# Spreading the pooling logits' maximum over all partitions by a store to DRAM and a load, in place of a diagonal, two products with ones and a copy

## The chip, the cores and the metric

The kernel runs on one core of one Trainium2 chip. What counts is the device time of one execution in microseconds (us). The kernel before was timed in three runs; one further execution was recorded by the hardware profiler, and every trace row below comes from that execution. Engine names are those of the profile: PE is TensorE (PEld its weight loads), DVE is VectorE, ACT is ScalarE, POOL is GpSimd, and SP is SyncE, which here only issues DMAs.

## The reference, cut to what matters

```
batch, n_heads, seq, head_dim = 8, 8, 576, 64;  n_mem = 32
a   = phi - max(phi, axis=2)                 # per (batch, head, memory slot), over the sequence
a   = exp(a);  a = a / (sum(a, axis=2) + 1e-9)
k_m = einsum('bhsm,bhsd->bhmd', a, k)        # pooling: 576 keys become 32
v_m = einsum('bhsm,bhsd->bhmd', a, v)
scores = q @ k_m^T / sqrt(64);  attn = softmax(scores)
x   = (attn @ v_m), heads side by side       # 4608 x 512
h   = x @ w_in                               # 512 -> 2048
out = (h - tanh(h)) @ w_out                  # 2048 -> 512
```

The change concerns the first line of the pooling softmax alone: the maximum of `phi` over the 576 positions, for each of the 256 pairs of head and memory slot of one batch, and how that maximum reaches the place where it is subtracted.

## The kernel before, in words

The 4608 tokens are cut into 18 units of 256. For each unit `u` and each quarter `fb` of the 2048 hidden features there is one slot: `mm1` (L572, into the PSUM tile `hs`), a polynomial for h - tanh(h) that goes ACT, DVE, ACT, DVE, ACT, POOL (L579, L587, L592, L597, L603, L608), three sums for a fast product on DVE (`f`, L621), and the second product (`mm2_blocks`, L708 and L715), which works on the slot two back. Values are split in a high and a low half of 16 bits, so there are several products for each. The first part of the kernel (up to about 225 us) is written out word by word in `START`. From then on a loop runs over slots 18 to 71, and `tasks` says which attention steps of a batch go into which slot.

A slot has three places for such steps: `do(0)` after `mm1`, `do(1)` after `mm2_blocks`, `do(2)` at the end of the slot. `PLAN` gives the steps of batches 4 to 7 by slot, counted from the slot of the batch's first token (36, 44, 52 and 60): in a string, words ahead of `;` go to the first place, words behind `;` to the second, words behind `|` to the third. `in_order` ties every engine to the order in which the program issues its instructions, so an engine, the DMA issue on SP included, never passes a waiting instruction.

The steps of one batch that matter here:

- `FQ`, `FA` (-11): the logits are loaded twice, as `pt` (partition = pair, 576 positions along the row, L102, into a buffer of the ring `q`, which has two) and as `e` (partition = position, 256 pairs along the row, L106).
- `X` (-10, second place): DVE takes the maximum of each row of `pt` (`mx`, 128 partitions by 2, L146) and multiplies the identity by it (`dg`, a diagonal for each of the two halves, L148).
- `KR..0` (same place, behind `X`): SP issues the first two key/value loads (L126, ring `q`) and the tail `kt` (L119).
- `XP` (-9, third place): one matrix product of a matrix of ones with `dg` (L157) puts the 256 maxima on every partition of the PSUM tile `pmx`. In the trace it is two pairs of weight load and product, since the operands are 32 bits.
- `YM` (same place): ACT copies `pmx` to the SBUF tile `ms` (L178), and POOL subtracts it from `e` in three instructions (L162 and twice L168).
- `YE` (-8, second place): ACT takes the exponential of `e` (L182).
- `V..0`, `KR..1`, `V..1` (-7): PE pools keys and values (`pkv`, L220 and L228). The second two key/value loads reuse the buffers of the first two, so SP issues them once `V..0` has read those.

Batches 0 and 1 subtract the maximum in another layout, and batches 2 and 3 are issued by `START` and `PLAN3`; none of these four is touched. The PSUM tile `pmx` comes from the pool `ps_a`, which has one buffer, shared with `pkv`, `pp` (L524) and others. The tiles `dg`, `ms` and the second half of a batch's queries share the one SBUF buffer of tag `qt`.

Of the kernel before, what the change touches and what calls it, by code (L numbers as in the profile page):

```python
# [8 lines left out]
F32 = mybir.dt.float32  # L9
# [4 lines left out]
AF = mybir.ActivationFunctionType  # L14
# [4 lines left out]
P = 128  # L19
# [66 lines left out]

class Attention:


    def __init__(self, tc, c, big, ps_a, ins):  # L90
        self.tc, self.c, self.big, self.ps_a, self.ins = tc, c, big, ps_a, ins
# [51 lines left out]
    def top(self, b, d):  # L143
        nc, big = self.tc.nc, self.big
        mx = big.tile([P, 2], F32, tag="mx", name=f"mx{b}")
        nc.vector.tensor_reduce(mx, d["pt"], axis=AX.X, op=ALU.max)  # L146
        dg = big.tile([P, 2, P], F32, tag="qt", name=f"dg{b}", bufs=1)
        nc.vector.tensor_tensor(  # L148
            dg, self.c["ident"].unsqueeze(1).to_broadcast((P, 2, P)),
            mx.unsqueeze(2).to_broadcast((P, 2, P)), op=ALU.mult,  # L150
        )
        d["dg"] = dg

    def top_all(self, b, d, ps=None):
        nc, dg = self.tc.nc, d["dg"]
        pa = self.psum(f"pmx{b}", ps)
        nc.tensor.matmul(pa[:, 0, 0:256], self.c["ones"], dg.rearrange("p a b -> p (a b)"), start=True, stop=True)  # L157
        d["px"] = pa
# [15 lines left out]

    def expo_pool(self, b, d):

        m = self.big.tile([P, 256], F32, tag="qt", name=f"ms{b}", bufs=1)
        self.tc.nc.scalar.activation(m, d["px"][:, 0, 0:256], AF.Copy)  # L178
        self.less_top(self.tc.nc.gpsimd, d["e"], m)

    def expo_exp(self, b, d):
        self.tc.nc.scalar.activation(d["e"], d["e"], AF.Exp)  # L182
# [155 lines left out]
def split_path(ctx, tc, c, ins, out):  # L338
    nc = tc.nc
# [5 lines left out]
    ps_o = ctx.enter_context(tc.tile_pool(name="ps_o", bufs=1, space=PSUM))  # L345
    ps_a = ctx.enter_context(tc.tile_pool(name="ps_a", bufs=1, space=PSUM))
    dram = ctx.enter_context(tc.tile_pool(name="part", bufs=1, space=bass.MemoryType.DRAM))
# [3 lines left out]
    wout_hi = const.tile([P, 16, DM], F16, name="wout_hi")  # L351
    wout_lo = const.tile([P, 16, DM], F16, name="wout_lo")
    att = Attention(tc, c, big, ps_a, ins)

    RING = {"gg": 3, "h3": 2, "uu": 2, "q": 2, "sc": 2}
    raws = {}
# [131 lines left out]
    st = [dict() for _ in range(B)]  # L488
# [306 lines left out]
    def early(b):  # L795
        return ps_early if b == 0 else None

    def cubic(u, fb, stay):
# [11 lines left out]
        "KA": lambda b: att.load_kv(b, st[b], (0,)), "KB": lambda b: att.load_kv(b, st[b], (1,)), "Q": lambda b, t: att.load_q(b, st[b], t, "q"), "QT": lambda b, t: att.load_q(b, st[b], t, "qt"),  # L810
        "KR": lambda b, r: att.load_kv_half(b, st[b], r),
        "X": lambda b: att.top_bias(b, st[b]) if b < N_ROWS else att.top(b, st[b]), "YX": lambda b: att.expo_rows(b, st[b]),
        "XT": lambda b: att.expo_turn(b, st[b], early(b), ps_o), "XP": lambda b: att.top_all(b, st[b], early(b)),
        "Y": lambda b: att.expo(b, st[b]), "YM": lambda b: att.expo_pool(b, st[b]), "YE": lambda b: att.expo_exp(b, st[b]),
        "V": lambda b, r: att.pool_half(b, st[b], r, st[b]["pk"] if r else None), "N": lambda b, r=None: att.norm(b, st[b]) if r is None else att.norm_half(b, st[b], r),
        "U": lambda b: att.turn(b, st[b], early(b)), "UV": att_turn_v, "W": att_window,
# [24 lines left out]
    for word in START.split():  # L841
        if ":" in word:
            k, tag = word.split(":")
# [3 lines left out]


    PLAN = (
# [241 lines left out]
@with_exitstack  # L1091
def tile_kernel(ctx: ExitStack, tc: tile.TileContext, qt, kva, kvt, pha, phx, w_in, w_out, out):
    nc = tc.nc
    ins = dict(qt=qt, kva=kva, kvt=kvt, pha=pha, phx=phx, w_in=w_in, w_out=w_out)
    const = ctx.enter_context(tc.tile_pool(name="const", bufs=1))
    c = {"first": len(nc.cur_bb.bb.instructions)}
    for name, shape, dt in (
        ("ident", [P, P], F32), ("ones", [P, P], F32), ("ones16", [P, 1], F16), ("one", [P, 1], F32),
        ("beta", [P, 1], F32), ("idw", [P, P], F32), ("nidp", [P, P], F16), ("idw", [P, P], F32), ("nid16", [P, P], F16), ("stat", [P, N_CHECK], F32), ("bad", [P, 1], I32),
    ):  # L1100
        c[name] = const.tile(shape, dt, name=name)
    make_identity(nc, c["ident"])
    nc.vector.tensor_scalar(c["nid16"], c["ident"], -1.0, None, op0=ALU.mult)
    nc.vector.tensor_scalar(c["nidp"], c["ident"], -S_V * S_W / S_P, None, op0=ALU.mult)
    nc.vector.tensor_scalar(c["idw"], c["ident"], S_W, None, op0=ALU.mult)
    nc.gpsimd.memset(c["ones"], 1.0)
    nc.gpsimd.memset(c["ones16"], 1.0)
    nc.gpsimd.memset(c["one"], 1.0)
    nc.gpsimd.memset(c["beta"], BETA)
    with ExitStack() as inner:  # L1110
        split_path(inner, tc, c, ins, out)
    with tc.If(c["wide"] > 0):
        with ExitStack() as inner:
            wide_path(inner, tc, c, ins, out)
# [39 lines left out]
```

## Time and profile before

| | |
|---|---|
| median of 3 runs | 659.96 us (659.03 to 661.41) |
| profiled execution: own time | 659.43 us |
| profiled execution: span of the trace | 657.6 us |
| granted PE clock, mean | 0.995 |
| busy DVE, ACT, POOL over the span | 523.6, 375.8, 251.0 us |
| bytes moved by DMA | 84.98 MB |

The span reaches from the first to the last recorded instruction; the execution's own time is 1.83 us longer. A timeline row gives the start in us, how long the row's instructions took together (first start to last end), engine, line, operation, the tile written and the tiles read, and how many instructions the row holds; in brackets stands how long the engine was idle just before, and what ended that. Matmuls overlap, so a row of one product lasts longer than the step to the next product's start.

### The profile page before, as it was taken

To read this page: it belongs to the slowest core of one execution; us is meant where nothing else is said; L and a number is where in the kernel's file an instruction comes from. 1 tells how busy PE (TensorE), PEld (TensorE's weight loads), DVE (VectorE), ACT (ScalarE), POOL (GpSimd) and SP (SyncE) were. 2 spreads that over 40 slices of the span, in tenths; PEclk is the share of its full clock that TensorE was granted. 3 is DMA by queue.
4 is the path that set the end of the run, shared out by engine and by line. 5 is a ranking of instruction groups with operands and counts; after the bars stand their busy time and mean duration, and the time that the engine had idled before them with its cause. 6 is when DMAs were issued, how large, how long until landed. Compare 5 with 4: busy or idle time off the path is not lost.

```text
span 657.6 us, 15599 instructions
## 1 busy us (share of the span) xinstructions
PE 642.2 (98%) x6690; PEld 456.3 (69%) x6690; DVE 523.6 (80%) x790; ACT 375.8 (57%) x509; POOL 251.0 (38%) x173
## 2 busy tenths in 40 slices
PE   8889999999999999999999999999999999999996
PEld 4355656566557777777776677877687777887885
DVE  6899999999855787875898679777978686867773
ACT  4577686666424456545655466545654677666541
POOL 0225141222222245451535353624452555455531
PEclk9899999999999999999999999999999999999999
DMA  9999345301423301324331515142415333234201
GB/s 343 377 365 393 109 170 180 117 3 65 146 97 102 138 28 74 113 91 145 105 113 66 168 51 168 37 162 70 146 41 197 98 101 117 63 117 136 86 33 37
DMA packets 25996, 84.98 MB, mean 129 GB/s; under 512 B 2880, under 2 KB 2880, under 8 KB 25152
## 3 DMA queue, kind: packets, MB, share of 16 engines
q1 hardware_dynamic: 24624, 81.55, 35.9%
q10 hardware_dynamic: 1296, 2.36, 0.9%
q8 instruction: 54, 0.88, 0.6%
q14 instruction: 22, 0.18, 0.1%
HBM read 72.37 MB, written 11.53 MB: 128 GB/s over the span
## 4 chain that ended last, share of the span: by engine, by line
PE 79%; DVE 11%; DMA 4%; ACT 2%; issue 2%; POOL 1%; SPq 0%; DVEq 0%; ACTq 0%; POOLq 0%
PE hs L572 20%; PE x L715 13%; PE o L708 13%; PE o L715 10%; PE o L651 6%; PE h L572 4%; PE o1h L651 3%; PE pp L524 3%; DMA raw<-in_w_out_dram 2%; PE pkv L220 2%; DMA kv<-in_kva_dram 2%; PE warm L789 1%; DVE wt L384 1%; DVE h L597 1%; DVE h L587 1%
## 5 line engine op out<-in xcount | busy, mean ns | idle before, releaser
L608 POOL TENSOR_TENSOR g<-h,g 128x1024 f16<-128x1024 f32 x64 | 138.5, 2165 | 327.3 <-ACT g L603 233.3
L572 PEld LDWEIGHTS <-ph 128*128 128x128 f16 x2304 | 176.9, 98 | 20.5 <-issue 6.0
L572 PE MATMUL hs<-ah,ph 128*128 128x256 f16 (+3 forms) x1152 | 151.5, 246 | 0.0
L587 DVE SCALAR_TENSOR_TENSOR h<-hs,u 128x1024 f32<-128x1024 f32 x54 | 65.8, 1219 | 91.0 <-ACT u L579 90.9
L603 ACT ACTIVATE g<-h 128x1024 f16<-128x1024 f32 x72 | 75.9, 1055 | 92.3 <-DVE h L597 90.2
L572 PE MATMUL hs<-al,ph 128*128 128x256 f16 (+3 forms) x576 | 127.6, 246 | 0.0
L592 ACT ACTIVATE u<-u,beta 128x1024 f32<-128x1024 f32 x72 | 82.4, 1147 | 55.5 <-DVE h L587 54.4
L708 PE MATMUL o<-wout_hi,g 128*128 128x512 f16 x432 | 104.7, 379 | 0.0
L715 PEld LDWEIGHTS <-f 128*128 128x128 f16 x896 | 87.7, 98 | 10.1
L597 DVE SCALAR_TENSOR_TENSOR h<-u,h 128x1024 f32<-128x1024 f32 x72 | 87.4, 1216 | 0.8 <-ACT u L592 0.7
L579 ACT ACTIVATE u<-hs 128x1024 f32<-128x1024 f32 x54 | 55.0, 1019 | 52.8 <-PE hs L572 48.3
L715 PEld LDWEIGHTS <-g 128*128 128x128 f16 x672 | 64.2, 98 | 26.5 <-issue 5.1
L715 PE MATMUL x<-bt,f 128*128 128x256 f16 x672 | 82.5, 273 | 0.0
L708 PEld LDWEIGHTS <-g 128*128 128x128 f16 x432 | 40.5, 98 | 43.9 <-issue 8.1
L621 DVE TENSOR_TENSOR f<-g 128x512 f16<-128x512 f16 x112 | 65.7, 626 | 4.3 <-POOL g L608 3.4
L651 PEld LDWEIGHTS <-g 128*128 128x128 f16 x384 | 36.7, 98 | 46.5 <-issue 3.4
L651 PE MATMUL o<-wout_hi,g 128*128 128x512 f16 x192 | 58.8, 379 | 0.0
L572 PE MATMUL h<-ah,ph 128*128 128x256 f16 (+3 forms) x384 | 49.6, 246 | 0.1
L572 PE MATMUL h<-al,ph 128*128 128x256 f16 (+2 forms) x192 | 42.4, 246 | 0.2 <-POOL al L515 0.2
L542 DVE SCALAR_TENSOR_TENSOR ph<-pp,ph 128x1024 f16<-128x1024 f32 x31 | 37.6, 1213 | 0.6 <-ACT ph L537 0.6
L537 ACT ACTIVATE ph<-pp 128x1024 f16<-128x1024 f32 x32 | 32.5, 1017 | 7.5 <-PE pp L524 7.4
L651 PE MATMUL o<-wout_lo,g 128*128 128x512 f16 x96 | 36.4, 379 | 0.0
(146 smaller groups left out, 980.0 us busy)
## 6 DMA issues: line engine op xcount, KB each, us to landing
kv<-in_kva_dram SPq DMA_DIRECT2D x20, 516.0 KB, 4.1
q<-in_qt_dram SPq DMA_DIRECT2D x16, 576.0 KB, 4.9
chk<-in_w_in_dram SPq DMA_DIRECT2D x16, 512.0 KB, 5.7
chk<-in_w_out_dram SPq DMA_DIRECT2D x16, 512.0 KB, 3.4
out_dram<-r SPq DMA_DIRECT2D x27, 256.0 KB, 2.4
kv<-in_kva_dram SPq DMA_DIRECT2D x6, 1032.0 KB, 8.8
raws<-in_w_in_dram SPq DMA_DIRECT2D x12, 512.0 KB, 7.1
raw<-in_w_out_dram SPq DMA_DIRECT2D x12, 512.0 KB, 7.2
```

Of the source, the lines that this page charges most:

```text
L542: nc.vector.scalar_tensor_tensor(pl, pa, S_P / (S_V * S_W), ph, op0=ALU.mult, op1=ALU.subtract)
L572: nc.tensor.matmul(hp[:, k, tu : tu + w], px[:, g, cs], d[ax][:, g, ta : ta + w], start=(n == 0), stop=(n == 5),)
L579: nc.scalar.activation(uu, hp, AF.Square, scale=1.0 / (S_A * S_P))
L587: nc.vector.scalar_tensor_tensor(h3, hp, C2 * S_G / (S_A * S_P), uu, op0=ALU.mult, op1=ALU.mult)
L592: nc.scalar.activation(uu, uu, AF.Square, bias=c["beta"])
L597: nc.vector.scalar_tensor_tensor(h3, uu, CC, hp, op0=ALU.add, op1=ALU.mult)
L603: nc.scalar.activation(gg[:, 0], h3, AF.Copy)
L608: eng.tensor_tensor(gg[:, 1], h3, gg[:, 0], op=ALU.subtract)
L621: nc.vector.tensor_tensor(o, x, y, op=op)
L651: nc.tensor.matmul(o, gx[:, k, P * tt : P * tt + P], wx[:, 4 * fb + k, :], start=(first and k == 0 and wx is wout_hi and gx is gh), stop=( ...
L708: nc.tensor.matmul(o[th], gg[:, 0, k, P * th : P * th + P], wout_hi[:, 4 * fb + k, :], start=(first and k == 0), stop=False)
L715: nc.tensor.matmul(dst, a(1 - n, kk), b(n, kk), start=(new and kk == 0 and n == 0), stop=(end and kk == 1 and n == 1))
```

## The change

For batches 4 to 7, `X` no longer builds the diagonal: SP stores `mx` (128 partitions by 2) into a DRAM tile of 2 rows by 128, turned, so that neighbouring partitions lie 4 bytes apart. A new step `XL`, in the first place of slot -9, has SP load that DRAM tile to all 128 partitions as `ms`. `XP` is gone from `PLAN`, and `YM` no longer copies on ACT. The subtraction on POOL is the same, in the same place.

```diff
     def top(self, b, d):
         ...
         nc.vector.tensor_reduce(mx, d["pt"], axis=AX.X, op=ALU.max)
+        if b > 3 and self.dram:
+            d["mx"] = self.dram.tile([2, P], F32, tag=f"mx{b}", name=f"mxd{b}")
+            nc.sync.dma_start(d["mx"].rearrange("a p -> p a"), mx)
+            return
         dg = big.tile([P, 2, P], F32, tag="qt", name=f"dg{b}", bufs=1)
         ...
+
+    def load_top(self, b, d):
+        d["ms"] = self.big.tile([P, 2, P], F32, tag="qt", name=f"ms{b}", bufs=1)
+        self.tc.nc.sync.dma_start(d["ms"], d["mx"].unsqueeze(0).to_broadcast((P, 2, P)))
+        d["ms"] = d["ms"].rearrange("p a x -> p (a x)")

     def expo_pool(self, b, d):
 
-        m = self.big.tile([P, 256], F32, tag="qt", name=f"ms{b}", bufs=1)
-        self.tc.nc.scalar.activation(m, d["px"][:, 0, 0:256], AF.Copy)
-        self.less_top(self.tc.nc.gpsimd, d["e"], m)
+        self.less_top(self.tc.nc.gpsimd, d["e"], d["ms"])
...
+    att.dram = dram
...
-        (-11, "FQ{0} FA{0}"), (-10, "; X{0} KR{0}0"), (-9, "| XP{0} YM{0}"), (-8, "; YE{0}"), ...
+        (-11, "FQ{0} FA{0}"), (-10, "; X{0} KR{0}0"), (-9, "XL{0} | YM{0}"), (-8, "; YE{0}"), ...
```

On PE, between the second product of one slot and `mm1` of the next, batch 4; before (`o` is the output's PSUM tile, `f` the sums, `ph` and `ah` the operands of `mm1`):

```order
L715 LDWEIGHTS f_3470
L715 MATMUL o_3476<-wout_lo,f_3470 128x256
L157 MATMUL pmx_3628<-dg_3517,ones 128x256
L572 LDWEIGHTS ph_2956
L572 MATMUL hs<-ah_3117,ph_2956 128x256
```

and now (the line numbers are 10 higher):

```order
L725 LDWEIGHTS f_3470
L725 MATMUL o_3476<-wout_lo,f_3470 128x256
L582 LDWEIGHTS ph_2956
L582 MATMUL hs<-ah_3117,ph_2956 128x256
L582 LDWEIGHTS ph_2956
```

The product with `ones` is gone, and `mm1` follows the second product directly; DVE loses the row of `dg` behind its `mx` and ACT the copy into `ms` in the same way, and nothing else moves on these engines, for each of the four batches. POOL's rows stay as they are.

On SP, which issues the DMAs one behind the other, from the last stores of a unit's output to the second pair of key/value loads of batch 4; before:

```order
L781 DMA out_dram<-r_3332 128x512
L126 DMA kv_3519<-in_kva_dram 128x1032
L126 DMA kv_3521<-in_kva_dram 128x1032
L119 DMA kt_3523<-in_kvt_dram 128x516
L126 DMA kv_3755<-in_kva_dram 128x1032
```

and now:

```order
L791 DMA out_dram<-r_3332 128x512
L151 DMA mxd_3517<-mx_3515 128x2x1
L128 DMA kv_3519<-in_kva_dram 128x1032
L128 DMA kv_3521<-in_kva_dram 128x1032
L121 DMA kt_3523<-in_kvt_dram 128x516
L162 DMA ms_3582<-mxd_3517 128x256
L128 DMA kv_3753<-in_kva_dram 128x1032
```

The store of the maxima (`mxd`) stands ahead of the first key/value load, the load of `ms` behind `kt` and ahead of the second pair.

More of the change, by code (lines that the diff above doesn't have):

```diff
@@ L87 @@
 class Attention:
+    dram = None
     def __init__(self, tc, c, big, ps_a, ins):
@@ L812, in split_path @@
         "X": lambda b: att.top_bias(b, st[b]) if b < N_ROWS else att.top(b, st[b]), "YX": lambda b: att.expo_rows(b, st[b]),
-        "XT": lambda b: att.expo_turn(b, st[b], early(b), ps_o), "XP": lambda b: att.top_all(b, st[b], early(b)),
+        "XT": lambda b: att.expo_turn(b, st[b], early(b), ps_o), "XP": lambda b: att.top_all(b, st[b], early(b)), "XL": lambda b: att.load_top(b, st[b]),
         "Y": lambda b: att.expo(b, st[b]), "YM": lambda b: att.expo_pool(b, st[b]), "YE": lambda b: att.expo_exp(b, st[b]),
```

2 rows, old and new, of the table PLAN are left out of this document.

## The prediction

> **What bounds the kernel now.** I read the page first: busy times, then the chain that ended last.
>
> ```profile
> span 657.6 us, 15599 instructions
> PE 642.2 (98%) x6690; PEld 456.3 (69%) x6690; DVE 523.6 (80%) x790; ACT 375.8 (57%) x509; POOL 251.0 (38%) x173
> PE 79%; DVE 11%; DMA 4%; ACT 2%; issue 2%; POOL 1%; SPq 0%; DVEq 0%; ACTq 0%; POOLq 0%
> ```
>
> PE is busy for 98% of the span and makes 79% of the chain. Busy alone may hide waits, so I next took the view by stages, for the stretch in which batches 4 to 7 are pooled. The columns are the stretch, its length, then busy time (instructions) of PE, PEld, DVE, ACT and POOL, the granted clock, the DMA share and GB/s:
>
> ```profile
> 300.00:400.00 100.00, 99.01 (x1000) 73.36 (x998) 79.63 (x120) 57.53 (x81) 44.79 (x29) 1.00 0.31 103
> 400.00:500.00 100.00, 99.70 (x1187) 75.23 (x1185) 84.03 (x123) 55.71 (x71) 45.31 (x31) 1.00 0.32 104
> 500.00:600.00 100.00, 99.66 (x1121) 78.03 (x1119) 71.87 (x110) 67.27 (x98) 49.23 (x34) 1.00 0.35 114
> ```
>
> PE has at most 1 us in 100 free, at full clock. The view of waits, from 225 to 600 us, says what those are (total us, times, longest):
>
> ```profile
> PE pkv L220 <- DMA kv<-in_kva_dram: 1.3, 2, 1.0
> PE pp L524 <- ACT wn L483: 0.3, 1, 0.3
> ```
>
> Two waits for the second pair of key/value loads, one short one for ACT, none for DVE, POOL or the diagonal. So a piece taken out of PE's row ends the kernel that much earlier, and time taken off DVE or ACT ends nothing earlier.
>
> **What is removed from PE.** The timeline of PE around the product with ones, for the first of the four batches and then the last:
>
> ```profile
> 275.37 0.27 PE L715 MATMUL o<-wout_hi,f 128*128 128x256 f16 x1
> 275.48 0.27 PE L715 MATMUL o<-wout_lo,f 128*128 128x256 f16 x1
> 275.59 0.60 PE L157 MATMUL pmx<-dg,ones 128*128 128x256 f32 x2
> 276.02 0.27 PE L572 MATMUL hs<-ah,ph 128*128 128x256 f16 x1
> ```
>
> ```profile
> 479.92 0.27 PE L715 MATMUL o<-wout_hi,f 128*128 128x256 f16 x1
> 480.02 0.27 PE L715 MATMUL o<-wout_lo,f 128*128 128x256 f16 x1
> 480.13 0.60 PE L157 MATMUL pmx<-dg,ones 128*128 128x256 f32 x2
> 480.57 0.22 PE L572 MATMUL hs<-ah,ph 128*128 128x128 f16 x1
> ```
>
> From one 16-bit product of 256 columns to the next PE steps 0.11 us (275.37 to 275.48), and from the last `o` to the first `hs` as well where nothing stands between, as at the end of the next slot:
>
> ```profile
> 283.32 0.27 PE L715 MATMUL o<-wout_lo,f 128*128 128x256 f16 x1
> 283.43 0.27 PE L572 MATMUL hs<-ah,ph 128*128 128x256 f16 x1
> ```
>
> Without `pmx` the first `hs` of batch 4's slot would so start at 275.59; it starts at 276.02. So the pair holds PE for 276.02 - 275.59 = 0.43 us, in the last batch for 480.57 - 480.13 = 0.44 us. Four batches: 4 x 0.435 = 1.74 us. No wait stands ahead of the pair, so nothing else is set free with it.
>
> **What is removed from DVE and ACT.** Their rows, with the stretch from the maximum to the pooling, in batch 4 and then batch 7 (DVE, ACT, POOL and PE, each from its own timeline):
>
> ```profile
> 270.14 1.31 DVE L146 TENSOR_REDUCE mx<-pt 128x2 f32<-128x1152 f32 x1
> 271.48 1.63 DVE L148 TENSOR_TENSOR dg<-ident,mx 128x256 f32<-128x256 f32 x1
> ...
> 277.84 0.37 ACT L178 ACTIVATE ms<-pmx 128x256 f32<-128x256 f32 x1
> ...
> 283.67 1.17 ACT L182 ACTIVATE e<-e 128x1152 f32<-128x1152 f32 x1 [1.31 <-POOL e L168]
> ...
> 278.01 2.13 POOL L608 TENSOR_TENSOR g<-h,g 128x1024 f16<-128x1024 f32 x1 [3.76 <-ACT g L603]
> 280.10 2.35 POOL L162 TENSOR_TENSOR e<-e,ms 128x1024 f32<-128x1024 f32 x1
> ...
> 286.14 0.43 PE L220 MATMUL pkv<-kv,e 128*32 128x129 f32 x8
> ```
>
> ```profile
> 473.49 1.31 DVE L146 TENSOR_REDUCE mx<-pt 128x2 f32<-128x1152 f32 x1
> ...
> 485.75 2.36 POOL L162 TENSOR_TENSOR e<-e,ms 128x1024 f32<-128x1024 f32 x1
> ...
> 489.34 1.17 ACT L182 ACTIVATE e<-e 128x1152 f32<-128x1152 f32 x1 [1.79 <-POOL e L168]
> ...
> 491.68 0.82 PEld L220 LDWEIGHTS pkv<-kv,e 128*32 128x32 f32 x32
> ```
>
> DVE loses 4 x 1.63 = 6.5 us and ACT 4 x 0.37 = 1.5 us. I take both at nothing: PE waits for neither here. POOL's subtraction starts when POOL is done with `g` (278.01 + 2.13 = 280.14), not when the copy is (278.21), so it doesn't start earlier either. Freeing the PSUM buffer of `pmx` sooner is worth nothing for the same reason: no row of PE waits for it.
>
> **What is added: the way through DRAM.** No store this small and no such load is in the trace. The rows nearest to them are a DMA store and reload of partial sums and the loads that now run beside it; columns: count, KB of each, us from issue to landing. Then SP's own timeline around batch 4's key/value loads, and the row of SP's queue (packets, MB, share of 16 engines over the span):
>
> ```profile
> d<-ot ACTq DMA_DIRECT2D x8, 256.0 KB, 2.1
> pr<-d SPq DMA_DIRECT2D x8, 256.0 KB, 3.2
> kt<-in_kvt_dram SPq DMA_DIRECT2D x8, 258.0 KB, 5.3
> ```
>
> ```profile
> 264.01 7.80 SPq L126 DMA_DIRECT2D kv<-in_kva_dram  x2
> 271.87 0.42 SPq L119 DMA_DIRECT2D kt<-in_kvt_dram  x1
> 287.26 0.81 SPq L126 DMA_DIRECT2D kv<-in_kva_dram  x2
> ```
>
> ```profile
> q1 hardware_dynamic: 24624, 81.55, 35.9%
> ```
>
> The chain from the end of `mx` to `ms` is: issue 0.42, store 2.1, issue 0.42, load 3.2, together 6.1 us. With the load landing only as late as `kt`, behind the key/value loads issued just ahead of it, it is 0.42 + 2.1 + 0.42 + 5.3 = 8.2 us. The store is 256 pieces of 4 bytes, for which the 2.1 is only a floor; a mean packet of this queue takes 0.359 x 16 x 657.6 / 24624 = 0.153 us of one engine, so 256 spread over 16 engines add at most 16 x 0.153 = 2.4 us if a small packet costs as much as a mean one of 3.3 KB. That would make 8.5 to 10.6 us. I take 7 us, between the reload row and the `kt` row.
>
> The cover: in batch 4 `mx` ends at 271.45 and POOL wants `ms` at 280.10, 8.65 us later; in batch 7 it is 485.75 - 474.80 = 10.95. Behind that, PE's `pkv` starts 286.14 - 284.84 = 1.30 us after ACT's exponential ends in batch 4, and 491.68 - 490.51 = 1.17 in batch 7. So PE waits only if the way takes over 9.95 us in batch 4, or over 12.1 in batches 5 to 7, which have the longer cover (batch 7's is taken for all three). At 7 us the price is nothing; at 10.6 us it is 0.65, once.
>
> SP has two new waits. At the store it waits for `mx` with the first key/value load behind it, which went out at 264.01 and will go out at about 272.3. Its reader `V` starts at 286.14, so some 10 us remain beyond a landing of about 4; price nothing. The second load waited for `mx` already (the two rows took 7.80 us). At the load of `ms` SP waits for the store to land; behind it stand only the loads of 287.26, which wait for `V` anyway.
>
> The Trainium skill, "DMA: Bandwidth & Descriptors", section "Rules for kernel authors", speaks against such a store: a strided last dimension becomes one descriptor per element, and small transfers pay mostly overhead. By its section "Anatomy of one DMA", about 2.0 us fixed for each DMA, my estimate of the way would be 2 x 2.0 us and the issues, about 4.9 us, and the sum would be the same; no row here shows 4-byte pieces.
>
> **The sum.** 659.43 - 1.74 = 657.7 us for the profiled execution. That execution was 0.53 us under the median of the runs; carried to the median, 659.96 - 1.74 = 658.2 us, 0.26% less. About 0.3% (2.0 us) is what a measurement of this kernel can tell from no change.
>
> **The rivals.**
> - *The sum as above, 0.78.* Its own spread comes from the 1.3 us that PE waits for key/value loads: if those waits vanish in the new execution the gain is 3.0 us; if all four batches wait the longest 1.0, it is 1.74 - 2.7 = -1.0. Of the 0.78, I put 0.25 beyond 2.0 us gained, 0.52 within 0.3%, 0.01 beyond on the other side.
> - *The products hold PE for their whole busy time, 0.09.* Then the gain is 8 x 0.385 = 3.1 us, 656.9 us, 0.47%.
>
> ```profile
> L157 PE MATMUL pmx<-dg,ones 128*128 128x256 f32 x12 | 3.6, 385 | 0.0
> ```
>
>   Against it: neighbouring 16-bit products last 0.27 us and step 0.11, so busy times overlap. The Trainium skill, "Trainium Kernel Development and Optimization", section "Performance Expectations", calls matmul busy time a bad metric because matmuls are pipelined; by that rule this rival is out, and the step of 0.11 agrees.
> - *The way through DRAM is late, slower, 0.08.* One mechanism: the 256 pieces of the store land late, POOL's subtraction, ACT's exponential and then `pkv` on PE follow. It eats the gain and 2.0 us more when (x - 9.95) + 3 (x - 12.1) = 1.74 + 2.0, that is from x = 12.5 us on. If the pieces went through one DMA engine, 256 x 0.153 = 39 us would come on top, and four batches would lose some 4 x 34 = 136 us, about 794 us. For it: no row bounds the small pieces from above. Against it: 16 engines share every transfer of 128 rows in this trace's queue.
> - *Nothing moves, 0.05.* Something that the trace doesn't show takes PE's 1.74 us back, the issue of the next weight load for instance: 660.0 us. Against it: at 283.43 `hs` follows `o` with the plain step.
>
> **How the numbers follow.** Faster by over 0.3%: 0.25 + 0.09 = 0.34. Within 0.3%: 0.52 + 0.05 = 0.57. Slower: 0.01 + 0.08 = 0.09. The range runs from the rival of the full busy time, 656.9, rounded to 656.8, to the sum's own worst end, 659.96 + 1.0, cut to 660.6 since four longest waits at once are unlikely.
>
> **What would show it.** Right: no `pmx` on PE after 225 us and `hs` one step of 0.11 behind `o` in the four places; `ms` landing within 9 us of the end of `mx`; POOL's subtraction still directly behind its forerunner; PE's stretches at 99% as now; the key/value waits between 0 and 4 us. Wrong: POOL waiting for the load of `ms`, `pkv` waiting for ACT's exponential, a wait of PE for the first key/value load, or a step of PE between `o` and `hs` that is longer than 0.11.

## The result, and the profile after

The changed kernel takes 682.06 us (median of 5 runs, 680.27 to 682.96) against 659.96 before (5 runs): a ratio of 1.0328, 95% interval 1.0309 to 1.0347. It is 3.3% slower; 658.2 was forecast. The profiled execution took 680.27 us, with a span of 678.4.

From the page of the changed kernel, busy times and the granted clock by slices:

```profile
span 678.4 us, 15578 instructions
PE 645.9 (95%) x6682; PEld 458.6 (68%) x6682; DVE 515.2 (76%) x786; ACT 374.2 (55%) x505; POOL 250.0 (37%) x173
...
PEclk9999999999999999979998999999997999999999
```

PE was busy for 642.2 us of 657.6 and is now busy for 645.9 of 678.4. So it stands still for 32.5 us where it stood 15.4, and although the four pairs of products are gone (6682 instructions in place of 6690) its busy time has grown by 3.7: something made its instructions longer. The clock row has dips to 7, 8 and 7. The view of waits from 225 us to the end (total us, times, longest) names the standing:

```profile
PE pkv L229 <- ACT e L191: 17.0, 4, 5.9
POOL e L173 <- DMA ms<-mxd: 12.5, 2, 7.2
POOL e L173 <- issue: 9.4, 2, 5.5
```

All four batches are there. POOL waits for `ms` (two of the four waits are put down to "issue", since the profile found no releaser for them), ACT for POOL, PE for ACT. Before, none of these rows existed for PE. The DMA view of the same stretch (count, KB of each, median us to landing) shows what is late:

```profile
ms<-mxd SPq DMA_DIRECT2D x4, 128.0 KB, 6.6
...
mxd<-mx SPq DMA_DIRECT2D x4, 1.0 KB, 8.7
```

The store of 1 KB takes 8.7 us to land, the load behind it 6.6. The key/value loads issued in between are late too. Batch 4 in the two DMA views, before (262 to 290 us) and after (271 to 290):

```profile
kv<-in_kva_dram SPq DMA_DIRECT2D x4, 516.0 KB, 3.8
...
kt<-in_kvt_dram SPq DMA_DIRECT2D x1, 258.0 KB, 4.2
```

```profile
kv<-in_kva_dram SPq DMA_DIRECT2D x2, 516.0 KB, 11.9
kt<-in_kvt_dram SPq DMA_DIRECT2D x1, 258.0 KB, 12.8
ms<-mxd SPq DMA_DIRECT2D x1, 128.0 KB, 7.2
mxd<-mx SPq DMA_DIRECT2D x1, 1.0 KB, 8.3
```

And the way itself in batch 4, row by row from the timelines of DVE, SP, POOL, ACT and PE:

```profile
270.90 1.31 DVE L148 TENSOR_REDUCE mx<-pt 128x2 f32<-128x1152 f32 x1
...
272.24 0.39 SPq L151 DMA_DIRECT2D mxd<-mx  x1
...
280.62 0.33 SPq L162 DMA_DIRECT2D ms<-mxd  x1
...
287.91 2.34 POOL L173 TENSOR_TENSOR e<-e,ms 128x1024 f32<-128x1024 f32 x1 [7.23 <-DMA ms<-mxd]
...
291.21 1.16 ACT L191 ACTIVATE e<-e 128x1152 f32<-128x1152 f32 x1 [8.50 <-POOL e L179]
...
292.43 1.95 PE L229 MATMUL pkv<-kv,e 128*32 128x129 f32 x32 [5.88 <-ACT e L191]
```

`mx` ends at 270.90 + 1.31 = 272.21. The store is issued at 272.24 and lands 8.3 us later, at 280.5; the load is issued at 280.62 and lands 7.2 us later, at 287.8; POOL starts at 287.91. The way is 287.91 - 272.21 = 15.7 us. POOL was free at 287.91 - 7.23 = 280.68 and stood for 7.23, ACT for 8.50, and PE, with its own slack of 1.30, for 5.88.

PE's other three waits, and the stretches behind all four in the view of windows (stretch, length, busy time of PE, PEld, DVE, ACT, POOL, granted clock, DMA share, GB/s):

```profile
366.19 1.95 PE L229 MATMUL pkv<-kv,e 128*32 128x129 f32 x32 [4.41 <-ACT e L191]
...
438.37 1.09 PE L229 MATMUL pkv<-kv,e 128*32 128x129 f32 x32 [2.63 <-ACT e L191]
...
510.66 1.95 PE L229 MATMUL pkv<-kv,e 128*32 128x129 f32 x32 [4.05 <-ACT e L191]
```

```profile
292.20:298.00 5.80, 5.57 (x50) 3.96 (x51) 3.57 (x6) 3.28 (x5) 2.13 (x1) 0.53 0.40 132
...
366.10:372.00 5.90, 5.81 (x59) 4.29 (x60) 3.81 (x6) 3.71 (x6) 3.25 (x2) 0.72 0.41 141
...
438.30:441.00 2.70, 2.63 (x47) 2.27 (x48) 0.79 (x1) 1.88 (x3) 1.60 (x1) 1.00 0.18 23
...
510.60:516.00 5.40, 5.34 (x49) 3.84 (x50) 3.34 (x5) 3.01 (x4) 3.25 (x2) 0.50 0.37 120
```

Behind the waits of 5.88, 4.41 and 4.05 us the granted clock is 0.53, 0.72 and 0.50, and the same 32 products of `pkv` take 1.95 us; behind the wait of 2.63 us the clock is 1.00 and they take 1.09. That is why PE's busy time grew. The Trainium skill, "TensorE: Matmul & The Clock Gate", section "Part 1: The HAM clock gate", has TensorE fall to half its clock after an idle window of about 3.4 us; these four rows agree, though in an experiment below half speed also followed a wait of 2.2 us.

The spans differ by 678.4 - 657.6 = 20.8 us. Of these PE's four waits are 17.0. The removed products give back 1.74, and the two waits for key/value loads of before (1.3) are gone. The changed execution was already 0.8 us later at the output stores of 263.79 (263.02 before), ahead of anything that the change touches. What is left is 20.8 - 17.0 + 1.74 + 1.3 - 0.8 = 6.0 us, which I put on the slow clock. The windows bound it from above: 0.47 x 5.80 + 0.28 x 5.90 + 0.50 x 5.40 = 7.1 us, if all work in these stretches went at the speed of the clock. PE's timeline shows it directly. From the first `pkv` to the next product of L718 the same work takes 292.43 to 297.69, 366.19 to 370.44 and 510.66 to 515.93 behind the three long waits, that is 5.26, 4.25 and 5.27 us; before (286.14 to 288.92) and behind the wait of 2.63 us (438.37 to 441.15) it takes 2.78. The excess is 2.48 + 1.47 + 2.49 = 6.4 us.

What was removed went as forecast. PE behind the second product, where `pmx` stood:

```profile
276.25 0.27 PE L725 MATMUL o<-wout_lo,f 128*128 128x256 f16 x1
276.36 0.27 PE L582 MATMUL hs<-ah,ph 128*128 128x256 f16 x1
```

`hs` follows `o` with the plain step of 0.11.

### The profile page after: what moved, and what is told of

Read it like the earlier page. It is cut to its first block, busy times and chain, and to the rows that moved or that the text cites. A ratio compares the mean times of both kernels' runs of the same rounds, so it can differ in the third digit from the quotient of the medians.

```text
span 678.4 us, 15578 instructions
## 1 busy us (share of the span) xinstructions
PE 645.9 (95%) x6682; PEld 458.6 (68%) x6682; DVE 515.2 (76%) x786; ACT 374.2 (55%) x505; POOL 250.0 (37%) x173
## 5 line engine op out<-in xcount | busy, mean ns | idle before, releaser
L718 PE MATMUL o<-wout_hi,g 128*128 128x512 f16 x432 | 104.8, 380 | 0.0
L725 PEld LDWEIGHTS <-f 128*128 128x128 f16 x896 | 89.2, 100 | 11.5
L725 PE MATMUL x<-bt,f 128*128 128x256 f16 x672 | 85.3, 278 | 0.0
L718 PEld LDWEIGHTS <-g 128*128 128x128 f16 x432 | 40.7, 98 | 44.2 <-issue 8.3
L631 DVE TENSOR_TENSOR f<-g 128x512 f16<-128x512 f16 x112 | 60.8, 584 | 4.3 <-POOL g L618 3.4
L229 PE MATMUL pkv<-kv,e 128*32 128x129 f32 x512 | 20.1, 303 | 18.3 <-ACT e L191 17.0
L547 ACT ACTIVATE ph<-pp 128x1024 f16<-128x1024 f32 x32 | 32.5, 1017 | 7.5 <-PE pp L534 5.1
```

Of the source, the lines that this page charges most:

```text
L631: nc.vector.tensor_tensor(o, x, y, op=op)
L718: nc.tensor.matmul(o[th], gg[:, 0, k, P * th : P * th + P], wout_hi[:, 4 * fb + k, :], start=(first and k == 0), stop=False)
L725: nc.tensor.matmul(dst, a(1 - n, kk), b(n, kk), start=(new and kk == 0 and n == 0), stop=(end and kk == 1 and n == 1))
```

## The experiments

The profile says that the way through DRAM is late, but not why the store needs 8.7 us. My theory at first: it is the 256 pieces of 4 bytes, and what is issued behind them is held up. Rivals: the store only shares its way with the 1.3 MB of key/value loads issued behind it; it is not how many pieces there are but where they lie in DRAM; or something else in the change costs the time. Times are compared by their ratio to the kernel before on the same chip (its medians there were 659.55 to 660.07). Lines shift by some rows from kernel to kernel.

### The load alone (no_store)

```diff
-            d["mx"] = self.dram.tile([2, P], F32, tag=f"mx{b}", name=f"mxd{b}")
-            nc.sync.dma_start(d["mx"].rearrange("a p -> p a"), mx)
             return
...
-        self.tc.nc.sync.dma_start(d["ms"], d["mx"].unsqueeze(0).to_broadcast((P, 2, P)))
+        self.tc.nc.sync.dma_start(d["ms"], self.ins["pha"][b, 0, 0:2].unsqueeze(0).to_broadcast((P, 2, P)))
```

> The changed kernel without the store: ms is loaded to all partitions from 1 KB of the logits input, at the same place of SP's queue; the maximum is still taken, and not used (any value per pair cancels in the softmax). Theory (the store of 4-byte pieces is what is late): with no store to wait for, ms is issued at about 274 us in batch 4 and lands within 7 us behind the key/value loads, POOL does not wait, pkv does not wait for ACT, and only the removal of the product is left: 659.96 - 1.74 = 658.2 us, between 657.0 and 659.5. Rival (the load of one KB to 128 partitions is itself slow): it lands 6 us after its issue even with an empty queue, and batch 4 still loses 0 to 2 us, 658 to 660. Rival (the removal is worth nothing): 660.0.

Measured: 656.90 us, ratio 0.9944 (0.9922 to 0.9966). The load's row in the DMA view:

```profile
ms<-in_pha_dram SPq DMA_DIRECT2D x4, 128.0 KB, 4.4
```

PE waits for neither the exponential nor a key/value load; the 0.3 us for ACT that stood there before is its only wait from 225 us on. The whole loss is gone with the store, and with POOL's dependence on it, which this kernel drops too (rows, below, keeps it); the new load, the new order on SP and the missing diagonal cost nothing. The gain is a little above what I had allowed: 657.6 - 654.5 = 3.1 us in span, which is the 1.74 of the products and the 1.3 of the key/value waits, which don't return.

### The key/value loads behind the way (kv_after)

```diff
-        ... (-10, "; X{0} KR{0}0"), (-9, "XL{0} | YM{0}"), ...
+        ... (-10, "; X{0}"), (-9, "XL{0} KR{0}0 | YM{0}"), ...
```

> The changed kernel with the first two key/value loads and the tail moved behind the load of ms in SP's queue, so that store and load have the DMA queue to themselves. Theory (the small pieces are slow by themselves): the store still lands 8 to 10 us after its issue; the load of ms, with nothing ahead of it, lands in 2 to 3 us; the way is 11 to 14 us against 16 now, so that batch 4 loses 1 to 4 us and the others 0 to 2, 659 to 667 us. Rival (the store is late because the key/value loads run beside it): it lands in 2 to 3 us, the way is 6 us and the time 658.2. Rival (the load is slow by itself): store 8 to 10, load 6 to 7, 678 to 682.

Measured: 672.64 us, ratio 1.0170 (1.0139 to 1.0202).

```profile
ms<-mxd SPq DMA_DIRECT2D x4, 128.0 KB, 6.2
...
mxd<-mx SPq DMA_DIRECT2D x4, 1.0 KB, 7.6
```

```profile
PE pkv L229 <- ACT e L191: 11.1, 4, 4.5
```

With nothing behind it in its queue until it has landed, the store still needs 7.6 us. Sharing with the loads is not its cause; that rival falls. My own expectation missed too: the load, now ahead of the key/value loads, takes 6.2 us where I had counted on 2 to 3. A load from the logits, with the loads around it, took 4.4.

### Other shapes of the store (forms)

The load is that of no_store, so the maxima are not used. In addition each batch issues one store that nobody waits for: 256 pieces of 4 bytes side by side (batch 4, as in the change), 256 pieces of 4 bytes 256 bytes apart (batch 5), 128 of 8 bytes side by side (batch 6), and 128 of 4 bytes 8 bytes apart (batch 7).

```diff
+            if b == 4:
+                t = self.dram.tile([2, P], F32, tag="fa", name="forma")
+                nc.sync.dma_start(t.rearrange("a p -> p a"), mx)
+            elif b == 5:
+                t = self.dram.tile([P, 128], F32, tag="fb", name="formb")
+                nc.sync.dma_start(t.rearrange("p (a x) -> p a x", a=2)[:, :, 0], mx)
+            elif b == 6:
+                t = self.dram.tile([P, 2], F32, tag="fc", name="formc")
+                nc.sync.dma_start(t, mx)
+            else:
+                t = self.dram.tile([P, 2], F32, tag="fd", name="formd")
+                nc.sync.dma_start(t[:, 0:1], mx[:, 0:1])
```

> As no_store, but each batch makes one store of its maxima to DRAM for which nobody waits, each in another form, at the place of the store of the changed kernel: batch 4 the 256 pieces of 4 bytes packed into 1 KB (as the changed kernel), batch 5 the 256 pieces of 4 bytes with 256 bytes from one to the next, batch 6 128 pieces of 8 bytes packed, batch 7 128 pieces of 4 bytes with 8 bytes from one to the next. Read from its profile alone: time to landing of each. Theory (number of pieces): 8 to 10, 8 to 10, 4 to 6, 4 to 6 us. Rival (pieces that share a short stretch of DRAM get in each other's way): batch 5 lands in 2 to 4 us, the others in 6 to 10. In both the key/value loads behind a slow store land late, as in the changed kernel (12 us).

Measured, once: 665.98 us. The DMA view from 225 us on, then that of batch 4 alone:

```profile
forma<-mx SPq DMA_DIRECT2D x1, 1.0 KB, 8.6
formb<-mx SPq DMA_DIRECT2D x1, 1.0 KB, 1.9
formc<-mx SPq DMA_DIRECT2D x1, 1.0 KB, 3.2
formd<-mx SPq DMA_DIRECT2D x1, 0.5 KB, 3.3
```

```profile
kt<-in_kvt_dram SPq DMA_DIRECT2D x1, 258.0 KB, 13.1
ms<-in_pha_dram SPq DMA_DIRECT2D x1, 128.0 KB, 14.2
```

This decides against my theory in its first form. The same 256 pieces with the same bytes land in 1.9 us when they lie 256 bytes apart and in 8.6 when they lie side by side. Half as many pieces in the same 1 KB take 3.2 or 3.3 us, whether they fill it or leave gaps. So in these four stores the time goes with how many pieces fall into one short stretch of DRAM. That each form stood in another batch is not what divides them: in the changed kernel the crowded store took as long in batches 5 to 7, from its issue to that of the load that waits for it, 355.41 - 345.42 = 10.0, 427.99 - 419.25 = 8.7 and 498.85 - 490.12 = 8.7 us. And the crowded store delays others without any dependence: in batch 4 nobody waits for it, and still `kt` and the independent load of `ms` land after 13.1 and 14.2 us; PE waited for ACT once, 6.4 us, in that batch. In batch 5, behind the spread store, they took 5.7 and 5.5.

### One slot earlier (early)

```diff
-        (-11, "FQ{0} FA{0}"), (-10, "; X{0} KR{0}0"), (-9, "XL{0} | YM{0}"), ...
+        (-11, "FQ{0} FA{0} ; X{0}"), (-10, "XL{0} ; KR{0}0"), (-9, "| YM{0}"), ...
```

> The changed kernel with the maximum and its store one slot earlier (second place of slot -11), the load of ms in the first place of -10, and the key/value loads behind it. One slot is about 8 us, so the cover grows from 8.6 to 11 us to 17 to 19 us. Theory: the way of 11 to 14 us (store 8 to 10, load 2 to 3) is covered in all four batches, no wait of pkv for ACT is left, and the time is that of the removal alone, 658.2 us (657.0 to 659.5). Rival (the store also disturbs other work, whoever waits for it): over 660.

Measured: 662.38 us, ratio 1.0033 (1.0019 to 1.0047), over the 657.0 to 659.5 that I expected and where the rival had it. The store still took 9.5 us, but PE's wait for it is nearly gone, and others stand in its place:

```profile
PE o L718 <- DVE r L790: 1.7, 4, 0.5
...
PE x L725 <- ACT u L589: 1.3, 3, 0.4
...
PE pkv L229 <- DMA kv<-in_kva_dram: 1.0, 2, 0.9
PE pkv L229 <- ACT e L191: 0.5, 1, 0.5
```

So cover can hide the store. But in the new slot the maximum of 1.3 us stands on DVE ahead of the additions for a unit's output (for one batch at 328.61, the additions of L790 at 332.53), which PE's next `o` needs. I had looked for free time ahead of the subtraction and not at what DVE owes PE in that slot. This accounts for the first row, 1.7 us; for the others I followed no chain, so the rival, that the store disturbs other work whoever waits for it, isn't excluded here. The four rows make 4.5 us; the 2 us that the span of 661.2 lies above 657.6 - 1.74 - 1.3 + 4.5 = 659.1 I could not place.

### Turned before the store (rows)

DVE turns the maxima by a 32 x 32 transpose, and two stores of four pieces of 128 bytes go out.

```diff
+            mw = big.tile([P, 32], F32, tag="mw", name=f"mw{b}", bufs=1)
+            mt = big.tile([P, 2, P], F32, tag="qt", name=f"mt{b}", bufs=1)[:, 0, 0:32]
+            nc.vector.memset(mw, 0.0)
+            nc.vector.tensor_reduce(mw[:, 0:2], d["pt"], axis=AX.X, op=ALU.max)
+            nc.vector.transpose(mt, mw)
...
-            nc.sync.dma_start(d["mx"].rearrange("a p -> p a"), mx)
+            for i in range(2):
+                rows = mt.rearrange("(k j) x -> k j x", j=32)[:, i]
+                nc.sync.dma_start(d["mx"][i].rearrange("(k x) -> k x", x=32), rows)
```

> The changed kernel with the maxima turned on DVE first (the 32x32 block transpose of a 128x32 tile whose first two columns are the maxima), so that the DRAM tile is stored in two DMAs of four pieces of 128 bytes each in place of 256 pieces of 4 bytes; load, places and queue as in the changed kernel. Theory (pieces that share a short stretch of DRAM are what is slow): the stores land in about 2 us as the spread form did (1.9), the key/value loads are not held, ms is issued at about 275 us in batch 4 and lands 4 to 6 us later, at most 1 us of batch 4 is left as a wait of pkv: 656.9 of no_store plus 0 to 1.5, 656.9 to 658.5 us. Rival (any store to DRAM that is reloaded at once costs the wait, whatever its pieces): way still over 12 us, 670 to 682.

Measured: 656.91 us, ratio 0.9958 (0.9944 to 0.9972), as expected. SP's timeline in batch 4:

```profile
274.55 1.16 SPq L156 DMA_DIRECT2D mxd<-mt  x2
...
277.31 0.33 SPq L169 DMA_DIRECT2D ms<-mxd  x1
```

The load, which waits for both stores, is issued 277.31 - 274.55 = 2.8 us after the first of them, against 8.4 in the changed kernel. It lands after 4.7 us (median of the four), and PE has no wait for ACT's exponential.

### Pairs of maxima side by side (pairs)

The DRAM tile is 128 rows of 2, so each partition stores one piece of 8 bytes; the load is contiguous, and POOL reads `ms` with a step of two.

```diff
-            d["mx"] = self.dram.tile([2, P], F32, tag=f"mx{b}", name=f"mxd{b}")
-            nc.sync.dma_start(d["mx"].rearrange("a p -> p a"), mx)
+            d["mx"] = self.dram.tile([P, 2], F32, tag=f"mx{b}", name=f"mxd{b}")
+            nc.sync.dma_start(d["mx"], mx)
```

> The changed kernel with the DRAM tile as 128 pairs, so that each partition stores one piece of 8 bytes (the form that landed in 3.2 us with nobody waiting); the load is the same 1 KB to all partitions, and POOL reads it with a step of two. Theory: store 3 to 4 us, load 5.5 to 7 us behind the key/value loads, way 10 to 12 us: batch 4 loses 0.5 to 2 us, the others nothing: 657.5 to 660 us. If POOL reads the stepped operand slower (its subtraction over 2.4 us), up to 2 us more. Rival (the wait for a store is what costs, not its form): over 670.

Measured: 657.21 us, ratio 0.9951 (0.9934 to 0.9968), a little under the 657.5 to 660 expected, since batch 4 loses nothing either.

```profile
ms<-mxd SPq DMA_DIRECT2D x4, 128.0 KB, 5.9
...
mxd<-mx SPq DMA_DIRECT2D x4, 1.0 KB, 3.4
```

The 128 pieces of 8 bytes land in 3.4 us, here as the median of all four batches, much as form c did once. Way: 3.4 + 5.9 = 9.3 us, over POOL's 8.65 in batch 4 (POOL waits 0.83 us for `ms` there) and inside the 9.95 with PE's slack; PE waits for neither the exponential nor a key/value load.

### Turned, and first on DVE (rows_first)

The kernel of rows, with `X` in the first place of slot -10:

```diff
-        ... (-10, "; X{0} KR{0}0"), ...
+        ... (-10, "X{0} ; KR{0}0"), ...
```

> As rows, with the maximum and its stores in the first place of slot -10 in place of the second, some 4 us sooner, ahead of the sums f on DVE. Theory: the cover of batch 4 grows from 8.65 to 12 to 13 us, no wait of pkv for ACT is left, 656 to 657.5 us. Against it: 1.3 us more of DVE ahead of f and g in that slot; if PE then waits for DVE there (as in early, where the maximum met the output's additions on DVE), 658 to 662.

Measured: 658.94 us, ratio 0.9985 (0.9976 to 0.9994): more cover, and 0.3% slower than rows. PE has waits that rows doesn't have:

```profile
PE pp L541 <- DVE kvn L252: 1.0, 2, 0.6
```

With 0.8 us for a key/value load and 0.5 for ACT's exponential they make 2.3 us, against 2.0 between the medians. I expected DVE to be late in the slot of `X`, but the first of the two waits of this row is at 364.00, some 30 us behind batch 5's maximum (332.18); how the earlier place leads to it is not shown.

### PE kept warm during the wait (warm_fill)

The changed kernel, with 16 products of 512 columns that nobody reads ahead of each batch's `pkv`:

```diff
+        if b > 3 and r == 0:
+            w = self.c["nid16"]
+            for _ in range(16):
+                nc.tensor.matmul(pa[:, 1], w, w.unsqueeze(1).to_broadcast((P, 4, P)), start=True, stop=True)
```

> The changed kernel with 16 idle products of 512 columns (about 3.4 us, into a PSUM buffer that the pooling overwrites) on PE ahead of the first pooling product of batches 4 to 7, where PE waits 2.6 to 5.9 us for ACT. They fill the wait and move nothing else. Theory (a wait of 4 us and more is followed by some 5 us at half the granted clock, and this is the part of the loss that the waits don't make up): PE idles at most 2.5 us in a row, the granted clock stays at full speed after it, and the time falls by 3 to 5.5 us to 676.5 to 679 us. Rival (the slow clock has nothing to do with the idle stretch): 682, or over that.

Measured: 678.19 us, ratio 1.0276 (1.0262 to 1.0291), which is 0.0052 x 660 = 3.4 us less than the changed kernel. The waits from 225 us on, and batch 4's `pkv`:

```profile
PE pkv L233 <- ACT e L191: 5.2, 4, 2.2
...
PE pkv L233 <- DMA kv<-in_kva_dram: 1.5, 2, 0.9
```

```profile
291.12 1.22 PE L233 MATMUL pkv<-kv,e 128*32 128x129 f32 x32 [2.21 <-ACT e L191]
```

More work made the kernel faster. The 64 products step by 0.215 us each, 13.8 in all; with the 5.2 us of waits left PE is held for 19.0 us against 17.0, and another 1.5 by the key/value loads. So the clock gave back 3.4 + 2.0 = 5.4 us, or 6.9 with those loads. The two profiled executions, from which the waits are, lie only 678.4 - 676.5 = 1.9 us apart, which makes it 3.9 to 5.4. Not all of it came back: behind 0.61, 0.88 and 1.45 us of idle time `pkv` took 1.09 us, but in batch 4, behind 2.21, the products of the next slot stepped by 0.21 us where 0.11 is usual, and the work up to L722 took 291.12 to 295.52, 4.40 us where 2.78 is usual. By PE's rows 6.4 - 1.6 = 4.8 us came back, which agrees with the profiled executions; the medians put it somewhat higher.

### The store from ACT's queue (act_queue)

```diff
-            nc.sync.dma_start(d["mx"].rearrange("a p -> p a"), mx)
+            nc.scalar.dma_start(d["mx"].rearrange("a p -> p a"), mx)
```

> The changed kernel with the store of the maxima issued by ACT in place of SP, so that it goes through another DMA queue than the key/value loads behind it; the load of ms stays on SP, behind them, and waits for the store as before. Theory A (the store holds what is behind it in its own queue): the key/value loads land in 4 to 6 us as in before, ms finds the queue empty and lands in 2 to 5 us, way 12 to 14 us, 660 to 668 us. Theory B (the packed pieces hold the DMA engines or the memory, whichever queue the others come from): the key/value loads land late as in the changed kernel (11 to 13 us), ms in 6 to 7, and the time is within 3 us of 682.

Measured: 672.85 us, ratio 1.0198 (1.0176 to 1.0220), between the two expectations. Batch 4 in the DMA view:

```profile
kv<-in_kva_dram SPq DMA_DIRECT2D x1, 516.0 KB, 7.2
kt<-in_kvt_dram SPq DMA_DIRECT2D x1, 258.0 KB, 8.6
...
mxd<-mx ACTq DMA_DIRECT2D x1, 1.0 KB, 8.8
```

The store is as slow from another queue, and loads in SP's queue still take 7.2 and 8.6 us where they took 3.8 and 4.2 before. So the hold is not only the order within a queue. The same view, 270 to 290 us in 40 slices of 0.5, shows more:

```profile
DMA  0000095989930000000000000022300000000000
GB/s 0 0 0 0 0 124 124 248 281 328 368 112 4 0 0 0 0 0 0 0 0 0 0 0 0 23 88 82 102 0 0 0 0 0 0 0 0 0 0 0
```

By 276.5 us 0.79 MB have moved, which is all of these two loads (516 and 258 KB); then the engines stand until the load of `ms`. But `kt` lands at 272.18 + 8.6 = 280.8, beside the store's 271.79 + 8.8 = 280.6. So across queues it was the report of landing that came late, not the moving of the bytes, as far as the packets in the trace show. In the changed kernel, where the loads stand in the store's own queue, their bytes are late too: from 273 to 281 us only 0.35 MB move. The load of `ms`, issued into an empty queue, landed after 4.3 us (median; 2.9 to 5.8), as theory A had it. The hold is smaller than in the changed kernel, and the kernel's time doesn't separate the two, since ACT now stands for DVE's maximum ahead of its own work for 19.9 us in all:

```profile
ACT g L613 <- DVE mx L148: 19.9, 4, 5.0
```

### The two good stores with the loads behind (rows_kv_after, pairs_kv_after)

The kernels of rows and of pairs with the edit of kv_after.

> As rows (stores of 128-byte pieces), with the first two key/value loads behind the load of ms, so that the load has the DMA queue to itself, after stores that are not held. It tells why the load still took 6.2 us in kv_after. Theory (there it came in the wake of the packed store): it lands in 2 to 3.5 us here. Rival (1 KB read by 128 partitions from one place is slow by itself): 5 to 6.5 us. Time in both cases 656 to 658 us, as the cover holds either way; if the later key/value loads are late for their products, up to 2 us more.

> As pairs (128 pieces of 8 bytes), with the first two key/value loads behind the load of ms. Theory: store 3 to 3.5 us, load 2 to 4, way 6 to 8 us, inside batch 4's cover of 8.65; POOL no longer waits for ms (0.8 us in pairs) and the time is that of pairs or up to 1 us less, 655.8 to 657.5 us.

Measured: 656.80 us, ratio 0.9961 (0.9947 to 0.9975), and 656.66 us, ratio 0.9954 (0.9941 to 0.9966). The load of the first, then that of the second:

```profile
ms<-mxd SPq DMA_DIRECT2D x4, 128.0 KB, 4.2
```

```profile
ms<-mxd SPq DMA_DIRECT2D x4, 128.0 KB, 5.6
```

Neither differs from its parent in time, as there was hardly a wait left to remove. The store of pairs lands after 2.7 us here. Ahead of all loads `ms` still takes 4.2 us in the first, between the 2 to 3.5 of the theory and the 5 to 6.5 of the rival, and 5.6 in the second, over the 2 to 4 expected. Why a load of 1 KB to 128 partitions mostly needs over 4 us, and 6.2 behind the crowded store in its own queue, stays open. The four kernels rows, pairs, rows_kv_after and pairs_kv_after can't be told apart; each is 0.4 to 0.5% faster than the kernel before, and some 3.6% faster than the changed one.

## Why the prediction was wrong

- **What bounds the kernel, and what is removed: right.** PE's row set the end; the products were worth their 1.74 us, and the time off DVE and ACT ended nothing earlier (no_store shows both). The 1.3 us of key/value waits, which I held for the spread of the sum, went away in no_store and made the gain 3.1; that was the case with 3.0 us in the first rival. The rival of the full busy time forecast nearly the same number, 3.1, from another cause; but from the last `o` to `hs` it was 0.54 us (275.48 to 276.02) and is now 0.11, so 0.43 went and not 0.77, and it is out.
- **The failed step: "I take 7 us" for the way through DRAM.** It was 15.7 us in batch 4; in batches 5 to 7, from the end of `mx` to POOL's start, 361.67 - 345.39 = 16.3, 433.84 - 419.22 = 14.6 and 506.14 - 490.10 = 16.0. Inside it the term that fell is the store, "at most 2.4" us on top of 2.1: it took 8.7. With these 2.4 the prediction had 8.5 to 10.6 us for the way, and the 7 that it took leaves them out. I bounded a 4-byte piece by the mean cost of a piece of 3.3 KB, as if cost could only shrink with size. The forms show what was missing: where the pieces lie. The load was mis-sized too, 6.6 us in place of 3.2 (reload row) or 5.3 (`kt` row). The issues, 0.42 each, should not have been added: the landing column counts from the issue, as the load of 280.62 right behind 272.24 + 8.3 shows. The figure that I worked out from the fixed cost in the Trainium skill, "DMA: Bandwidth & Descriptors", section "Anatomy of one DMA", 4.9 us (its terms add to 4.8), was further off; that section measured DMAs issued from GpSimd, and these two go through SP's queue. The Trainium skill's rule on strided last dimensions, same page, section "Rules for kernel authors", pointed the right way, but form b is as strided and landed in 1.9 us, so that rule alone doesn't tell the slow store from the quick one.
- **The rival "late" was the right case, given 0.08.** Its thresholds held: with the four ways above, (15.7 - 9.95) + (16.3 - 12.1) + (14.6 - 12.1) + (16.0 - 12.1) = 5.75 + 4.2 + 2.5 + 3.9 = 16.4 us of waiting, and PE waited 17.0. I saw that no row bounds the small pieces from above, and then still let the range end at 10.6 us for the way.
- **Not priced: the clock after the wait,** about 6 us. The formula for that rival counted only PE's standing time. Behind each wait of over 4 us PE's products ran slow for 3 to 5 us more (in batch 5 0.28 x 5.90 / 0.5 = 3.3 us, in batch 4 up to 297.69, 5.3).
- **Wrong about the neighbours:** the first key/value loads were to land in about 4 us behind the store; they took 11.9 in batch 4. That cost PE nothing directly, since `ms` was later still, but kv_after, which takes these loads out of the way, waits 11.1 us in place of 17.0.

## What to carry to other kernels

When maxima or sums that lie one per partition go through DRAM, turn them to rows first, or at least store what a partition has as one piece, and look at the landing time of the store and of what is issued behind it. A transfer of a kind that the trace has never shown has no upper bound from the mean of other transfers: keep the range open on that side, or time it by itself first. Price a new wait of the matmul engine with the slow clock that follows it, and before moving work to an earlier slot see what the engine owes to others there.

## What the runs showed of the hardware that I had not expected

- A store of 256 pieces of 4 bytes landed in 8.6 us when they filled 1 KB of DRAM and in 1.9 us when they lay 256 bytes apart (one store each); 128 pieces in 1 KB took 2.7 to 3.4. What in the memory or the DMA engines does this, no run here shows.
- Such a store delays other transfers that don't depend on it, in its own queue (loads of 3.8 and 4.2 us took 11.9 and 12.8) and in another (7.2 and 8.6). In the other queue the bytes of both loads had moved by 276.5 us, and the second of them landed at 280.8.
- Idle times of PE of 4.05 us and more cost it half its clock for 3 to 5 us; one of 2.63 us didn't, one of 2.21 us was followed by half speed, so no single limit can be read from these runs. Filling such a wait with idle products gave back 3.4 us of 22.
